# Attention backward on one core: loads and stores queued four at a time, the compute plan around them, a warm-up and halved last stores

## The chip, the cores and the metric

The kernel runs on one core of a Trainium2 chip. The metric is device time in microseconds (us): the median over executions of one build. Kernels that were executed once (the two repeats, those with loads and stores alone, the probes, many_dma, dense_dma, vec_dma, tag_before) have the state "unknown", since there is nothing to compare them with; their differences of some us are not backed by repeats. A profiled execution gives a span; it was 1.7 to 1.8 us shorter than the time of the same execution in the two profiles that are shown.

## The reference, cut to what matters

Attention with 32 query heads over 4 key/value heads, and its gradients. There are 32 batches; per batch `k` and `v` are 4 heads x 2048 keys x 128 in bf16, and `q`, `grad_out` are 32 heads x 4 queries x 128.

```python
def _fwd_reference(q, k, v):
    ...
    k = jnp.repeat(k, rep, axis=1)          # rep = 8 query heads share a key/value head
    v = jnp.repeat(v, rep, axis=1)
    scores = jnp.einsum("bhqd,bhkd->bhqk", q, k) * D ** -0.5
    p = _softmax(scores, axis=-1)
    return jnp.einsum("bhqk,bhkd->bhqd", p, v)

def reference(q, k, v, grad_out):
    ...
    _out, _vjp = jax.vjp(_f, q, k, v)
    return (out, dq, dk, dv)
```

Per batch the kernel reads K and V (4.2 MB) and writes dK and dV (4.2 MB); `q`, `grad_out`, the output and dQ are small and travel as an extra 256 bytes at the end of some rows. In all, 272.65 MB cross between memory and the chip's on-chip buffer (SBUF).

## The kernel before: the parts that the change touches

Everything is written out in advance. A string, `PLAN`, lists units of four characters: the name of the unit, its part, where it goes (PSUM bank, engine or slot) and a tile. The units are emitted in that order, so PLAN fixes the order on every engine. About 101 units make a batch.

Twenty "row slots" in SBUF hold both the rows that are loaded (K, V) and the rows that are to be stored (dV, dK). Per batch there are four loads and four stores of 128 rows each, of 8,192 bytes a row (LV0, LV1, SV0, SK0) or 8,448 bytes (LK0, LK1, SV1, SK1). All are issued by SyncE (SP), in order.

```python
SLOTS, E_TILES, DS_TILES = 20, 2, 2
NAMES = dict(a="LK", b="LV", ..., r="O", ..., u="DP", ..., y="DQ", ..., B="DVe", ..., D="DKe", E="SV", F="SK")
PLAN = ("a000a110b120a030b040a150e400f4A0e011f0A0..." ...)      # cut
...
    def emit(u):
        ...
        if name in ("LK", "LV"):                       # a load into slot u.where
            x = slots[int(u.where, 36)]
            ...
            for w in (slice(0, Sk), slice(Sk, n)) if b == 0 else (slice(0, n),):
                nc.sync.dma_start(out=x[:, w], in_=src[:, w])
        ...
        elif name in ("O", "DQ"):                      # 64 matmuls of 32 rows x 128 columns a batch, each
            ...
            for c in range(8):
                j, odd = divmod(c, 2)
                for h, r in enumerate(rows):
                    right = t[x, h].rearrange("p (j d e) -> p j d e", d=D, e=2)
                    nc.tensor.matmul(t[name][r, :], lhsT=left[:, j, r, odd], rhs=right[:, 4 * i + j, :, odd],
                                     start=(i == 0 and c == 0), stop=(i == 1 and c == 7), tile_position=(0, 32 * h))
        ...
        elif name in ("DVe", "DKe"):                   # eviction: PSUM -> the row that will be stored
            i, g = divmod(i, 2)
            copy = nc.scalar.copy if u.where == "A" else nc.vector.tensor_copy
            copy(out=heads_of(t[name[:2], "out", g])[:, :, QW * i:QW * i + QW],
                 in_=t[name[:2], i, g].rearrange("p (h c) -> p h c", h=2))
        elif name in ("SV", "SK"):                     # a store, from the slot
            n = LONG if i else ROW
            nc.sync.dma_start(out=(dv_r if name == "SV" else dk_r)[i][b], in_=t["D" + name[1], "out", i][:, 0:n])
```

In the plan before, loads and stores alternate. The order on the queue in each batch is `LV1 LK0' SK1 SV1 LV0 SV0 LK1' SK0` (a prime marks a later batch), and each store stands directly behind its last eviction.

At most eight DMAs were outstanding. DMA k was issued only when all of DMA k-8 had landed (of the 252 from the ninth on, none starts earlier): LK1 of batch 25 was issued at 482.6 us, the moment at which LK1 of batch 24, eight DMAs earlier, landed (482.6 us).

## Time and profile before

| | before |
|---|---|
| time, median of 3 | 672.78 us (672.17 to 672.86) |
| profiled span | 671.1 us |
| TensorE (PE) busy | 607.9 us, 91% |
| VectorE, ScalarE (DVE, ACT) busy | 572.0 and 569.6 us |
| data, at the usual packet time (309 ns for 8,192 bytes, on 16 engines 424 GB/s) | 643 us |

The first fence is from the page of the profile: busy time and count of each engine, the strips of the span in 40 equal slices (a digit is tenths of busy time; GB/s is what the DMA engines moved), the DMA queues (packets, MB, share of 16 engines) and the chain of work that ended last.

```profile
span 671.1 us, 20678 instructions
...
PE 607.9 (91%) x8768; PEld 401.4 (60%) x8768; DVE 572.0 (85%) x736; ACT 569.6 (85%) x802; POOL 39.0 (6%) x102
...
DMA  9999999999999999999999999999999999999867
GB/s 354 417 424 423 419 381 423 423 423 423 423 426 424 424 423 424 424 425 426 414 420 425 413 417 421 414 422 424 396 388 408 417 424 424 404 421 423 347 258 322
...
q1 hardware_dynamic: 37440, 272.65, 98.2%
q8 instruction: 69, 1.13, 0.6%
...
DMA 50%; PE 37%; DVE 4%; ACT 4%; issue 3%; SPq 0%; POOL 0%; DVEq 0%; ACTq 0%; POOLq 0%
```

Read it so: the DMA strip is full until the last three slices, the rate is 424 GB/s in a good slice, and half of the chain is DMA. The line `q8` is not data of the kernel: 69 packets of 16,384 bytes (the packet records give the size), which the page lists as of the kind "instruction".

### The profile page before, as it was taken

To read this page: it belongs to the slowest core of one execution; us is meant where nothing else is said; L and a number is where in the kernel's file an instruction comes from. 1 tells how busy PE (TensorE), PEld (TensorE's weight loads), DVE (VectorE), ACT (ScalarE), POOL (GpSimd) and SP (SyncE) were. 2 spreads that over 40 slices of the span, in tenths; PEclk is the share of its full clock that TensorE was granted. 3 is DMA by queue.
4 is the path that set the end of the run, shared out by engine and by line. 5 is a ranking of instruction groups with operands and counts; after the bars stand their busy time and mean duration, and the time that the engine had idled before them with its cause. 6 is when DMAs were issued, how large, how long until landed. Compare 5 with 4: busy or idle time off the path is not lost.

```text
span 671.1 us, 20678 instructions
## 1 busy us (share of the span) xinstructions
PE 607.9 (91%) x8768; PEld 401.4 (60%) x8768; DVE 572.0 (85%) x736; ACT 569.6 (85%) x802; POOL 39.0 (6%) x102
## 2 busy tenths in 40 slices
PE   6998999999998999988998989988999989898993
PEld 5665566666665666655655655655655666565651
DVE  1988799999997999988888989887888979896994
ACT  4997899999997999888888989887888979886894
POOL 0000000000000000000000000000000000000000
PEclk9999999999998999999999999998999989998997
DMA  9999999999999999999999999999999999999867
GB/s 354 417 424 423 419 381 423 423 423 423 423 426 424 424 423 424 424 425 426 414 420 425 413 417 421 414 422 424 396 388 408 417 424 424 404 421 423 347 258 322
DMA packets 37533, 273.97 MB, mean 408 GB/s; under 512 B 4160, under 2 KB 4160, under 8 KB 5184
## 3 DMA queue, kind: packets, MB, share of 16 engines
q1 hardware_dynamic: 37440, 272.65, 98.2%
q8 instruction: 69, 1.13, 0.6%
q14 instruction: 24, 0.20, 0.1%
HBM read 136.31 MB, written 136.31 MB: 406 GB/s over the span
## 4 chain that ended last, share of the span: by engine, by line
DMA 50%; PE 37%; DVE 4%; ACT 4%; issue 3%; SPq 0%; POOL 0%; DVEq 0%; ACTq 0%; POOLq 0%
DMA row<-in_k_dram 50%; PE psum L241 19%; PE psum L310 8%; PE psum L288 5%; PE psum L255 5%; ACT row L316 3%; DVE vt_sb L209 2%; DVE ds_sb L303 1%; DVE row L316 0%; DVE e_sb L260 0%; ACT e_sb L264 0%; PE psum L230 0%; SPq L226 0%; ACT dt_sb L207 0%; DVE row L296 0%
## 5 line engine op out<-in xcount | busy, mean ns | idle before, releaser
L241 PE MATMUL psum<-ident,row 128*128 128x128 f32 x2048 | 290.1, 284 | 28.4 <-DMA row<-in_k_dram 21.5
L316 ACT CAST row<-psum 128x1024 bf16<-128x1024 f32 x292 | 289.2, 1023 | 30.9 <-PE psum L310 29.1
L241 PEld LDWEIGHTS psum<-ident,row 128*128 128x128 f32 x2048 | 224.7, 143 | 94.8 <-issue 32.0
L316 DVE CAST row<-psum 128x1024 bf16<-128x1024 f32 x220 | 264.9, 1217 | 5.7 <-PE psum L310 2.9
L207 ACT COPY kt_sb<-psum 128x512 f32<-128x512 f32 x190 | 110.2, 598 | 20.6 <-PE psum L241 20.4
L207 ACT COPY vt_sb<-psum 128x512 f32<-128x512 f32 x160 | 92.0, 602 | 35.3 <-PE psum L241 34.6
L303 DVE SCALAR_TENSOR_TENSOR ds_sb<-psum,delta,e_sb 128x1024 bf16<-128x1024 f32 x64 | 82.1, 1283 | 13.4 <-PE psum L255 9.0
L310 PE MATMUL psum<-ds_sb,qp_sb 32*128 32x512 bf16 x512 | 76.9, 383 | 3.4 <-ACT row L316 1.0
L260 DVE TENSOR_SCALAR_CACHE_REDUCE e_sb<-psum 128x2048 bf16<-128x2048 f32 x32 | 73.3, 2292 | 5.7 <-PE psum L255 5.7
L310 PE MATMUL psum<-e_sb,dop_sb 32*128 32x512 bf16 x512 | 68.8, 388 | 2.5 <-issue 1.0
L209 DVE COPY kt_sb<-psum 128x1024 bf16<-128x1024 bf16 x66 | 45.0, 685 | 28.4 <-PE psum L241 27.8
L209 DVE COPY vt_sb<-psum 128x1024 bf16<-128x1024 bf16 x96 | 60.7, 684 | 10.0 <-PE psum L241 9.8
L264 ACT ACTIVATE e_sb<-psum,m 128x2048 bf16<-128x2048 f32 x32 | 64.0, 2001 | 0.2 <-DVE e_sb L260 0.2
L271 POOL TENSOR_SCALAR dop_sb<-row,rinv 128x128 bf16<-128x128 bf16 x32 | 19.3, 603 | 605.3 <-DVE rinv L268 530.3
L241 PE MATMUL psum<-ident,ds_sb 128*128 128x128 f32 x256 | 41.8, 286 | 9.6 <-DVE vt_sb L209 7.0
L288 PE MATMUL psum<-row,dt_sb 128*32 128x128 bf16 x2048 | 43.5, 222 | 6.2 <-issue 5.6
L310 PEld LDWEIGHTS <-qp_sb 32*128 32x128 bf16 x512 | 19.4, 91 | 46.1 <-issue 42.6
L255 PE MATMUL psum<-vt_sb,qdt_sb 128*32 128x512 bf16 x512 | 40.7, 388 | 4.6 <-issue 4.5
L288 PEld LDWEIGHTS <-dt_sb 128*32 128x32 bf16 x2048 | 30.8, 95 | 22.0 <-issue 21.1
L241 PEld LDWEIGHTS psum<-ident,ds_sb 128*128 128x128 f32 x256 | 26.9, 140 | 27.2 <-DVE vt_sb L209 16.4
L207 ACT COPY dt_sb<-psum 128x512 f32<-128x512 f32 x63 | 38.4, 611 | 1.0 <-PE psum L241 0.9
L288 PEld LDWEIGHTS <-et_sb 128*32 128x32 bf16 x2048 | 30.4, 95 | 13.8 <-ACT et_sb L207 11.3
(29 smaller groups left out, 310.1 us busy)
## 6 DMA issues: line engine op xcount, KB each, us to landing
out_dram<-row SPq DMA_DIRECT2D x64, 1056.0 KB, 20.1
out_dram<-row SPq DMA_DIRECT2D x64, 1024.0 KB, 20.4
row<-in_k_dram SPq DMA_DIRECT2D x62, 1056.0 KB, 18.1
row<-in_v_dram SPq DMA_DIRECT2D x62, 1024.0 KB, 20.5
row<-in_v_dram SPq DMA_DIRECT2D x4, 512.0 KB, 9.4
row<-in_k_dram SPq DMA_DIRECT2D x2, 544.0 KB, 5.3
row<-in_k_dram SPq DMA_DIRECT2D x2, 512.0 KB, 4.4
```

Of the source, the lines that this page charges most:

```text
L207: nc.scalar.copy(out=out.bitcast(FP32), in_=in_)
L209: nc.vector.tensor_copy(out=out, in_=in_.bitcast(BF16))
L241: nc.tensor.transpose(out=ps[:, P * j:P * j + P], in_=src[:, 4 * half + j, :], identity=ident32[:])
L255: nc.tensor.matmul(out[r, QW * w:QW * w + QW], lhsT=t["qdt"][:, P * side + 32 * h:P * side + 32 * h + 32], rhs=t[x, NH * i + h][:, QW * w: ...
L260: nc.vector.tensor_scalar(out=t["e"][:], in0=t["S"], scalar1=-scale, scalar2=None, op0=ALU.mult, op1=ALU.min, accum_out=t["m"][:])
L264: nc.scalar.activation(out=t["e"][:], in_=t["S"], func=ACT.Exp, bias=t["m"][:], scale=scale, accum_out=t["l"][:])
L271: nc.gpsimd.tensor_scalar(out=t["dop"][:], in0=t["go"], scalar1=t["rinv"][:], scalar2=None, op0=ALU.mult)
L288: nc.tensor.matmul(t[name][r, :], lhsT=left[:, j, r, odd], rhs=right[:, 4 * i + j, :, odd], start=(i == 0 and c == 0), stop=(i == 1 and c ...
L303: nc.vector.scalar_tensor_tensor(out=t["ds"][:, w], in0=t["DP", i], scalar=t["dl"][:], in1=t["e"][:, w], op0=ALU.subtract, op1=ALU.mult)
L310: nc.tensor.matmul(acc[:, QW * (h % 2):QW * (h % 2) + QW], lhsT=t[still][rows[h], :], rhs=t[moving][rows[h], QW * i:QW * i + QW], start=Tr ...
L316: copy(out=heads_of(t[name[:2], "out", g])[:, :, QW * i:QW * i + QW], in_=t[name[:2], i, g].rearrange("p (h c) -> p h c", h=2))
```

## The change

The intent, as far as the plan shows it: fewer changes of direction on the DMA queue. Four loads of a batch are queued in a row, then four stores: `LK0 LV0 LV1 LK1 | SV0 SV1 SK0 SK1`. Three of the four stores of a batch are held back for that (most of them 46, 70 or 91 units behind their last eviction, before: 1; SK1 still stands directly behind its last piece, the eviction of dQ), and compute is ordered anew, with long runs of the matmuls of O, DQ and DP placed where the loads run. Twenty transposes at the start are meant to warm PE up (in before the first 24 transposes took 228 to 243 ns each and the next 20, from 12.0 us on, 119), the first batch's loads are no longer halved, the last batch's stores are halved, and evictions write contiguous pieces. The diff, with the plan cut out:

```diff
+LAST = 31
+WARM_UP = 20
 ...
-PLAN = ("a000a110b120a030b040a150e400f4A0e011f0A0e702f7A0 ...")     # cut: all lines of the plan change
+PLAN = ("a000e000e111f1A0f0A0e422f4D0e533f5A0a110e744c050 ...")
 ...
+        if u.name in ("SV", "SK") and u.part > 1:
+            u.b = LAST
 ...
-            for w in (slice(0, Sk), slice(Sk, n)) if b == 0 else (slice(0, n),):
-                nc.sync.dma_start(out=x[:, w], in_=src[:, w])
+            nc.sync.dma_start(out=x[:, 0:n], in_=src)
 ...
-            copy(out=heads_of(t[name[:2], "out", g])[:, :, QW * i:QW * i + QW],
-                 in_=t[name[:2], i, g].rearrange("p (h c) -> p h c", h=2))
+            copy(out=t[name[:2], "out", g][:, 2 * QW * i:2 * QW * i + 2 * QW], in_=t[name[:2], i, g])
         elif name in ("SV", "SK"):
-            n = LONG if i else ROW
-            nc.sync.dma_start(out=(dv_r if name == "SV" else dk_r)[i][b], in_=t["D" + name[1], "out", i][:, 0:n])
+            half, g = divmod(i, 2)
+            n = LONG if g else ROW
+            w = (slice(0, n), slice(0, ROW // 2), slice(ROW // 2, n))[half]
+            nc.sync.dma_start(out=(dv_r if name == "SV" else dk_r)[g][b][:, w], in_=t["D" + name[1], "out", g][:, w])
 ...
+        for _ in range(WARM_UP):
+            nc.tensor.transpose(out=psum[:, QW * (BANKS - 1):QW * (BANKS - 1) + P], in_=ident32[:], identity=ident32[:])
```

The host's unpacking of dK and dV changes with the layout of the evictions. Slots are also reused sooner: a load follows the store that frees its slot by mostly 6 DMAs (before: 7 to 13), an eviction by mostly 5 or 6 (before: 9 to 14; the prediction counts one less, only the DMAs in between).

## The prediction

> **What bounds the kernel now.** The DMA engines. The page's strip shows them at 0.9 or more busy in 37 of 40 slices and about 424 GB/s in the good ones. The packet records agree: an 8192-byte packet takes 309 ns, on 16 engines 424 GB/s. [...] At that pace 272.65 MB take 643 us, of a span of 671.1. The compute engines have room: the starts of two successive exponentials lie 18.8 to 19.1 us apart where nothing stops them, against 20.1 us of DMA per batch; over most of the run the chain of waits is the DMA queue, about 20.5 us per batch.
>
> So at most some 28 us can go. I divide them by the packets' times:
> - start, 0 to 20 us: 3.0 us;
> - middle: about 11 us, nearly all of it packets that take longer than 309 ns, in bursts of 4 to 8 us (near 85-93, 475-480, 495-501 us) where the data rate falls by a fifth;
> - tail, from 620 us: 13.8 us, of which 12.5 are idle engines. The loads are over, the stores wait for evictions (timeline of the DMA queue's engine: one load at 619.3 us, then stores alone). The last store is issued at 663.1 us and waited for over 6.6 us.
>
> **What the change does.** Bytes, DMA count (apart from splits) and arithmetic stay. Evictions move between ACT and DVE, but with the measured durations (copies 0.60 and 0.69 us, casts 1.02 and 1.22 us) both engines' sums stay within 1%. The contiguous eviction target should not change a cast's time[...].
>
> 1. *Tail.* Counted in queue order at 424 GB/s, the last load ends at 610 us instead of 615 and the K loads of the last batch at 598 instead of 603: the last two batches' arithmetic starts about 5 us earlier. Half stores land sooner: the half loads at the start took 4.4 to 5.3 us, so the 6.6 us should become about 4.5. Gain 5 to 8 us.
> 2. *Start.* The transposes before 12 us take 228 to 243 ns each, later 119; the warm-up removes that. But the first load is no longer halved, and the DMA queue is full anyway: gain 0 to 1 us.
> 3. *Grouping.* Direction now changes twice per batch instead of some six times. Against it: where only loads ran (12 to 30 us) packets were about 1.3% over 309 ns, where only stores ran 2 to 3%, in the good mixed stretches 0.2%. For it: the bursts may come from mixing or from matmul runs meeting store reads; then part of 11 us goes. I expect these nearly to cancel: gain 0 to 6 us.
> 4. *Risk.* Slots are reused sooner (a load follows the store of its slot by 6 DMAs, before by 7 to 13; evictions into a slot follow its store by 4 or 5, before by 9 to 11), so compute waits for stores and the queue runs shallower; a loss only if it empties.
>
> **Prediction.** 662.5 us, 1.5% faster; 8 in 10 between 652 and 671. Chances: faster by over 2% 0.36, within 2% 0.59, slower by over 2% 0.05.
>
> **What would show it.** Tail: slices after 620 us above 340 GB/s on average, last store issued by about 658 us. Grouping: long packets in the middle fewer, or a common 313-317 ns pace in their place. Compute: exponentials still about 20.4 us apart or less, engine sums unchanged.
>
> **What would make it wrong.** Bursts vanish altogether (about 652), or the shallower queue empties each batch, or pure load and store phases are slower than read here (over 670).

A cast measured 1.02 us on ACT and 1.22 us on DVE in before and in after alike. Neither is a term of its sum, which stays as recorded: gains of 5 to 8, 0 to 1 and 0 to 6 us, together 5 to 15 us, and 662.5 us is some 10 us below before.

## More of the kernel before

The waits of SP, the issuer of all DMAs, say what held the queue back (total us, number of waits, longest):

```profile
SPq L320 <- DMA out_dram<-row: 125.1, 64, 2.2
SPq L226 <- DMA out_dram<-row: 105.4, 23, 5.6
SPq L320 <- DVE row L316: 89.1, 15, 9.3
```

Most of its waiting is for DMAs to land: in the first line for one of the eight places; in the second it is nearly always LK0, a load that waits for the store, seven DMAs ahead, that frees its slot. In the third a store stands at the head of the queue before its eviction is done. And the end of the run, by stage (length, busy time of each engine and number of instructions, granted clock, DMA share, GB/s):

```profile
600.00:640.00 40.00, 35.67 (x516) 23.88 (x515) 32.61 (x44) 32.18 (x45) 2.39 (x6) 0.96 0.94 392
640.00:671.10 31.10, 20.08 (x331) 11.48 (x329) 20.58 (x24) 21.60 (x29) 1.20 (x3) 0.89 0.68 278
642.00:646.00 4.00, 3.92 (x41) 2.64 (x40) 3.73 (x4) 3.44 (x7) 0.00 (x0) 1.00 0.74 304
646.00:650.00 4.00, 3.31 (x26) 1.83 (x25) 3.73 (x6) 4.00 (x6) 0.79 (x2) 1.00 0.09 34
```

From 640 us on the DMA engines are busy for only 68% of the time. The prediction took that as idle time to be won. The last of these lines already holds the answer, which I did not see at the time: from 646 to 650 us the DMA share is 0.09, a little over one engine of sixteen.

## The result, and the profile after

| | before | after |
|---|---|---|
| time, median of 4 runs of the same rounds | 672.47 us (671.41 to 672.86) | 676.75 us (676.19 to 678.05) |
| ratio | | 1.0069 (95% interval 1.0050 to 1.0088) |
| profiled span | 671.1 us | 674.9 us |

The kernel is slower, by about 4 us, and the interval excludes zero. Every ratio in this document is the mean time of one kernel's runs over the mean of the other's runs of the same rounds, so it is not quite the ratio of the medians that are quoted.

The page of after, the lines that answer to those shown of before:

```profile
span 674.9 us, 20722 instructions
...
PE 619.4 (92%) x8788; PEld 422.5 (63%) x8788; DVE 567.2 (84%) x760; ACT 575.3 (85%) x778; POOL 39.3 (6%) x102
...
DMA  9999999999999999999999999999999999999996
GB/s 365 420 418 423 389 424 423 422 425 427 422 422 424 425 423 423 418 398 411 419 402 425 409 416 412 412 424 407 415 416 392 389 424 358 422 403 343 344 422 280
...
q1 hardware_dynamic: 37440, 272.65, 98.7%
q8 instruction: 69, 1.13, 0.6%
...
PE 46%; DMA 34%; ACT 8%; DVE 5%; issue 5%; SPq 0%; POOL 0%; DVEq 0%; ACTq 0%
DMA out_dram<-row 29%; PE psum L244 24%; PE psum L313 10%; ACT row L319 6%; PE psum L291 6%; PE psum L258 5%; DMA row<-in_v_dram 3%; DMA row<-in_k_dram 2%; DVE vt_sb L214 2%; DVE row L319 1%; ACT row L297 1%; DVE ds_sb L306 1%; DVE e_sb L263 1%; PE psum L233 1%; DVE dt_sb L214 0%
```

The sums of DVE and ACT moved by 1% or less. PE's 11.5 us more go with a lower granted clock (the share of the full TensorE clock that the profile shows as allowed), 0.961 on average against 0.982: busy time times clock is 595 us here and 597 us before. The good slices still reach 424 GB/s, but there are fewer of them after the middle, and the share of the chain that is DMA is now stores (`out_dram<-row`), where it was loads before. The waits of SP and, new, waits of the two evicting engines for stores to land (there are none of these in before):

```profile
SPq L324 <- ACT row L297: 201.6, 27, 10.3
SPq L229 <- DMA out_dram<-row: 105.4, 46, 6.3
SPq L324 <- DVE row L319: 78.5, 27, 14.1
```

```profile
ACT row L319 <- DMA out_dram<-row: 24.3, 15, 2.2
...
DVE row L319 <- DMA out_dram<-row: 17.0, 15, 1.8
```

And the end by stage; the last load landed at 639.0 us (before: 640.1 us):

```profile
600.00:639.00 39.00, 38.16 (x556) 25.51 (x554) 33.57 (x45) 37.13 (x54) 2.20 (x5) 1.00 0.95 346
639.00:674.90 35.90, 22.88 (x409) 12.94 (x407) 22.99 (x29) 23.57 (x30) 1.42 (x4) 0.88 0.86 355
```

The tail is fuller than before (355 against 278 GB/s), exactly as the prediction wanted, and yet it is 4.8 us longer.

### Where the time is: the slowest of sixteen engines

The page averages over 16 DMA engines. The landings of the shares do not. The next table is worked out from them: for each DMA I took the time at which its last share landed, and from one DMA to the next the excess over 2.49 us (19.93 us a batch of eight DMAs, the pace that loads and stores alone kept, see below; half DMAs count half). It is thus the time that the slowest engine loses, waiting included, by the stage in which it loses it. That the sums come near to what the spans have over 643 us follows from the definition; what the table adds is where the time goes.

| us lost by the slowest engine, by stage of the span | 20-100 | 100-300 | 300-500 | 500-600 | 600-642 | from 642 | sum |
|---|---|---|---|---|---|---|---|
| before | 4.3 | 10.0 | 7.0 | 3.5 | 1.6 | 2.4 | 28.8 |
| before, second profile | 3.8 | 9.5 | 6.7 | 3.0 | 2.5 | 1.5 | 27.0 |
| after | 3.6 | 5.5 | 8.9 | 6.3 | 5.3 | 1.9 | 31.5 |
| after, second profile | 3.8 | 5.5 | 8.4 | 6.0 | 5.1 | 2.1 | 30.9 |
| loads and stores alone, order of before | 0.7 | 1.0 | 0.3 | 0.2 | -0.1 | 0.0 | 2.1 |

Three things follow.

First, the loss is no matter of a few bursts or of the two ends: in before it is 20.5 us over the 24 batches from 100 to 600 us, some 0.8 us a batch, where loads and stores alone lose 1.5 us. Second, after gains 4 to 4.5 us between 100 and 300 us, and gives back 7.3 to 8.4 us from 300 to 642 us. Third, the tail itself is not idle on that engine, in either kernel: from the last load's landing to the last store's, it works off its queue at 2.7 us a store, 11 stores before ((670.0 - 640.1) / 11 = 2.72) and 13 after ((673.8 - 639.0) / 13 = 2.68, the eight half stores counted as four). Before, the other engines are 7 to 13 us ahead of it (shares of the last load: first 626.6, fifteenth 632.8, last 640.1 us) and wait; that is the "idle" DMA time of the tail. From 642 us to the end that engine loses no more than 2.4 us in before: this is all that a better filled tail could have saved on it. The very last stores end nearly together on all engines (670.0 us on the slow one, 668.1 to 668.3 us on fourteen), since each is issued only when its evictions are done; so compute was close to being the limit there.

So after loads its last row 1.1 us earlier, but has two more stores still to do: 2 x 2.7 - 1.1 is 4.3 us, against 3.8 us of difference between the spans. This is bookkeeping and not yet a cause. The two stores merely changed places with loads: at the same place of the queue, 245 whole DMAs, the last share landed at 640.1 us in before and at 644.5 us in after. The time was lost before the tail.

Spread of the landings: in before, the distance from the first to the last share of a DMA grows from 2.3 us (batch 4) to about 12.8 us (batch 16) and stays there. From there on nearly each DMA is issued when the slowest engine frees a place, so all engines go at its pace (20.7 us a batch from batch 16 to 27, first and last share alike). In after the spread stays at about 7 us (5 to 9).

### The profile page after: what moved, and what is told of

Same layout as the page of the kernel before. It is cut to its first block, busy times and chain, and to the rows that moved or that the text cites. A ratio compares the mean times of both kernels' runs of the same rounds, so it can differ in the third digit from the quotient of the medians. Undisturbed runs are those within 1.5% of the kernel's fastest.

```text
span 674.9 us, 20722 instructions
## 1 busy us (share of the span) xinstructions
PE 619.4 (92%) x8788; PEld 422.5 (63%) x8788; DVE 567.2 (84%) x760; ACT 575.3 (85%) x778; POOL 39.3 (6%) x102
## 4 chain that ended last, share of the span: by engine, by line
PE 46%; DMA 34%; ACT 8%; DVE 5%; issue 5%; SPq 0%; POOL 0%; DVEq 0%; ACTq 0%
DMA out_dram<-row 29%; PE psum L244 24%; PE psum L313 10%; ACT row L319 6%; PE psum L291 6%; PE psum L258 5%; DMA row<-in_v_dram 3%; DMA row<-in_k_dram 2%; DVE vt_sb L214 2%; DVE row L319 1%; ACT row L297 1%; DVE ds_sb L306 1%; DVE e_sb L263 1%; PE psum L233 1%; DVE dt_sb L214 0%
## 5 line engine op out<-in xcount | busy, mean ns | idle before, releaser
L319 ACT CAST row<-psum 128x1024 bf16<-128x1024 f32 x349 | 341.8, 1022 | 46.5 <-DMA out_dram<-row 24.3
L244 PEld LDWEIGHTS psum<-ident,row 128*128 128x128 f32 x2048 | 233.5, 146 | 68.3 <-ACT row L319 33.4
L319 DVE CAST row<-psum 128x1024 bf16<-128x1024 f32 x163 | 197.9, 1219 | 21.1 <-DMA out_dram<-row 17.0
L214 DVE COPY kt_sb<-psum 128x1024 bf16<-128x1024 bf16 x117 | 80.2, 687 | 32.2 <-PE psum L244 21.5
L214 DVE COPY vt_sb<-psum 128x1024 bf16<-128x1024 bf16 x149 | 97.6, 685 | 11.0 <-PE psum L244 9.8
L313 PE MATMUL psum<-e_sb,dop_sb 32*128 32x512 bf16 x512 | 83.3, 398 | 19.8 <-ACT row L319 19.5
L212 ACT COPY kt_sb<-psum 128x512 f32<-128x512 f32 x139 | 79.6, 597 | 20.2 <-PE psum L244 20.0
L212 ACT COPY vt_sb<-psum 128x512 f32<-128x512 f32 x107 | 60.2, 599 | 7.4 <-PE psum L244 6.2
L313 PEld LDWEIGHTS <-dop_sb 32*128 32x128 bf16 x512 | 23.8, 92 | 51.8 <-issue 40.8
L291 PEld LDWEIGHTS <-dt_sb 128*32 128x32 bf16 x2048 | 33.8, 95 | 11.5 <-issue 6.7
L244 PE MATMUL psum<-ident,e_sb 128*128 128x128 f32 x256 | 39.4, 280 | 0.0
## 6 DMA issues: line engine op xcount, KB each, us to landing
out_dram<-row SPq DMA_DIRECT2D x62, 1056.0 KB, 12.8
```

What stands on the lines that cost most here:

```text
L212: nc.scalar.copy(out=out.bitcast(FP32), in_=in_)
L214: nc.vector.tensor_copy(out=out, in_=in_.bitcast(BF16))
L244: nc.tensor.transpose(out=ps[:, P * j:P * j + P], in_=src[:, 4 * half + j, :], identity=ident32[:])
L313: nc.tensor.matmul(acc[:, QW * (h % 2):QW * (h % 2) + QW], lhsT=t[still][rows[h], :], rhs=t[moving][rows[h], QW * i:QW * i + QW], start=Tr ...
L319: copy(out=t[name[:2], "out", g][:, 2 * QW * i:2 * QW * i + 2 * QW], in_=t[name[:2], i, g])
```

## The experiments

A letter for a theory holds for the runs of its own section; the theories changed as they fell. Eighteen kernels were run.

### 1. Chance or program: the two kernels again

> The kernel before once more, to see whether the stretched packets are a property of the program or chance. If they come from what the program does (addresses, order, slots), the same DMAs are slow again: the K loads of batches 18 to 23 and 25 to 27, and the excess over 309 ns per 8192 bytes sums to about 13.8 us per engine. If they come from outside, other DMAs are slow and the sum differs by some us. About 672 us either way.

> The changed kernel once more. If the program makes the stretched packets: again about 21 us per engine, and again the second K load (LK1) of every other batch from 16 on and the last store of every other batch. If chance: other DMAs, another sum. About 677 us.

Measured, on one chip: 671.88 us and 675.82 us. The second profiles lose their time in the same stages as the first (table above) and at the same DMAs (correlation of the losses, DMA by DMA from the 17th to the 250th: 0.82 for before, 0.92 for after), and the same two loads of batches 30 and 31 are late in both profiles of after. The difference belongs to the program.

### 2. The order of the DMAs alone

Each kernel cut down to its loads and stores, in its own order and slots; no compute, results wrong.

```diff
-    units = plan()
+    units = [u for u in plan() if u.name in ("LK", "LV", "SV", "SK")]     # as a plan of 256 or 260 units; slots are set to zero first
```

> The loads and stores of the kernel before alone, in its order and slots, no compute (wrong results on purpose). Theory Q (the order of the DMA queue, by itself, decides the rate): about 660 us, with the stretched packets still there. Theory C (the compute engines' accesses or their waits make the losses): 643 us of packets plus 3 to 5 us at the ends, 646 to 652 us, with almost no stretched packets.

> The loads and stores of the changed kernel alone, grouped four and four, no compute (wrong results on purpose). Theory Q: slower than the same for the kernel before by 4 us or more, because grouping stretches packets. Theory C: the same as that run within 2 us, so that the loss of the changed kernel arises in the interplay with compute (slots that are freed late, evictions that wait for stores).

Measured: 647.15 us and 649.83 us, 25 us less than with compute. The page of the first:

```profile
span 645.4 us, 365 instructions
...
GB/s 335 424 426 421 428 425 427 425 428 425 428 426 428 428 429 426 425 428 427 429 427 427 428 428 428 428 426 428 427 428 427 428 427 428 428 427 429 427 428 339
...
q1 hardware_dynamic: 37440, 272.65, 100.4%
q14 instruction: 2, 0.02, 0.0%
```

All 16 engines keep one pace, 19.93 us a batch. So the DMA engines did the whole job in spans of 645 and 648 us. After's order costs 2.5 us here, all of it in the first 300 us (the slowest engine loses 4.7 us up to 300 us, against 1.7 us in the order of before); its sooner reuse of slots is part of that run too, so this is not grouping alone, and each of the two kernels was executed once. And some 25 us of both kernels come from the presence of compute. The line of instruction fetches of PE, `q8`, is gone.

### 3. Are the held-back stores the cost?

After, with each store moved to directly behind its last eviction (89 stores moved, nothing else).

> The changed kernel with each store moved in the DMA queue to right behind its last eviction (91 stores or fewer move; nothing else). Theory H (stores are held back until the four loads are queued, so that finished outputs keep their slots and evictions and loads wait for stores that have not landed): the 41 us in which ACT and DVE wait for a store shrink below 10 us and the time falls to 668 us or less. Theory D (the order of directions itself is what costs): still grouped three and three, so within 2 us of 676.7. Theory P (packets are stretched by what compute does at the same moment): the sum of stretched time changes with the phase, up or down, and the time with it.

Measured: 732.39 us, ratio 1.0882 (1.0849 to 1.0916). The theory that holding the stores back costs time is refuted for this order of loads; there it saves 56 us. What happens instead is in SP's waits:

```profile
SPq L324 <- DVE row L319: 424.8, 62, 20.3
SPq L324 <- ACT row L319: 97.9, 57, 16.9
```

SP stands at a store whose eviction is not done, and the loads behind it in the queue wait with it. With four loads in a row, the loads have to come before stores that are not ready.

### 4. Grouping alone

Before, with three of the four loads of a batch moved to a later place so that four loads and four stores stand in a row; slots and compute untouched.

> The kernel before with three of four loads moved later in the DMA queue, so that four loads and four stores follow one another, slots and compute order untouched; a load follows the store of its slot by 12 to 18 DMAs. Theory D (grouping itself costs): 3 us or more slower than before, stretched time above 16 us against 13.8. Theory H: within 1.5 us of before, since no slot becomes tight.

Measured: 684.53 us, ratio 1.0181 (1.0161 to 1.0202). In the compute order of before, this grouping costs 12 us. It also brings three loads of each batch later, and the run does not separate the two. By the landings, the last load lands at 650.5 us instead of 640.1, and the rest takes 31.6 us instead of 31.0, so the loss lies before the tail. If grouping costs as much in after, its new compute order recovers most of it; that is a comparison, not a test.

### 5. Does one kind of matmul take the bandwidth?

The DMA stream of each kernel, with PE working through long runs of one kind of matmul after the other (S, O, DV, transposes), then evictions. Their outputs are wrong, which doesn't matter for the times.

> The DMAs of the kernel before alone, while the compute engines run one kind of work after the other on tiles of their own, without any wait on the DMAs (wrong results on purpose): about 100 us of S-type matmuls, 100 of O-type, then DV-type, transposes, evictions. Theory P (a kind of matmul or eviction takes SBUF or other bandwidth from the DMA engines): in one of these stretches the packets take well over 309 ns and the data rate falls by 10 per cent or more. Otherwise none of the stretches differs from the DMAs alone (0.76 us stretched in 500) and the time is 645 to 650 us.

> The same probe with the DMA order of the changed kernel, loads and stores in separate phases of 10 us. Theory P: the stretching in the affected stretch follows the direction, loads or stores, and shows which of the two suffers. Otherwise as the DMAs alone, 648 to 652 us.

Measured: 736.34 and 735.84 us, set by the evictions at the end, so the time says nothing. The DMA stream is what counts: its last share landed at 666 and 669 us, against 644 and 647 us without compute. The slowest engine lost 1 to 4 us in each 60 us of PE's work after 40 us, whatever its kind, and in the probe of before only 0.4 us after PE's work had ended (526 us). No kind of matmul stood out. That PE's work costs the DMA engines some 22 us, whatever the work is, was the new fact.

### 6. What of PE's work costs? Many small instructions, or few large ones

Here I rebuilt, from the packet records, which packets belong to one DMA engine: on a busy engine of these records a packet starts 3 or 4 ns before the one ahead of it ends, and the shares of the DMAs follow in order. For the run of loads and stores alone this puts exactly 2,340 packets on each of 16 chains. In before and after it shows two things that the page does not: the 69 fetch packets lie on eight of the engines in turn (in before a fetch took its engine 0.88 to 1.38 us, median 0.94, and the packet behind it some 0.4 us over its pace), and one other engine has many small delays of 2 to 40 ns (16 to 18 us in sum in the two profiles of before, 17.4 us in the second of after; each of the other 15 under 1.5 us).

Four kernels. The first two are the loads and stores of before with a stream of matmuls that wait for nothing:

```python
        for n in range(13800):                                     # many_dma: 32 x 32, 64 columns moved
            h = n % 4
            nc.tensor.matmul(psum[rows[h], ...], lhsT=vt[rows[0], 0:32], rhs=e[rows[0], 0:64], start=True, stop=True,
                             tile_position=(0, 32 * h))
        for n in range(3000):                                      # dense_dma: 128 x 128, 512 columns moved
            nc.tensor.matmul(psum[...], lhsT=vt[:, 0:P], rhs=e[...], start=True, stop=True)
```

> Only the loads and stores of the kernel before, in its order, plus 13,800 tiny matmuls on PE (32 rows by 32 columns, 64 columns moved) that wait for nothing; results wrong on purpose. Chaining the DMA packets of the run of before by their times puts each 16,384-byte instruction-fetch packet on one of eight of the sixteen engines in turn, and each costs that engine about 0.95 us plus about 0.4 us on the packet behind it. Theory F (instruction fetch slows the DMA engines): about 108 fetches, 13 or 14 on each of eight engines at about 1.3 us, so the last landing moves from 643.9 us (loads and stores alone) to 655-664 us, with no one engine that stands out by many small delays of 5 to 40 ns. Theory D (dense streaming of PE, not the number of its instructions, slows one single engine by many small delays): that signature is missing here (sum of delays of 2 to 40 ns under 5 us on every engine).

> The same loads and stores, plus 3,000 matmuls of 128 by 128 with 512 columns moved[...], so that PE streams for some 640 us with few instructions. Theory F: about 23 fetches, 3 on each of eight engines, last landing at most 649 us. Theory D: one engine alone shows small delays (2 to 40 ns a packet) of 15 us or more in sum, as one engine did in the profiles of before (16 to 18 us) and after (about 17 us), the other fifteen under 3 us, and the last landing is at 658 us or later, with the other engines some 10 us ahead or held back by it.

The third halves the number of matmuls of O and DQ in before, with PE as long at work (busy 606.6 us, before 607.9; wrong):

```diff
-            for c in range(8):
-                j, odd = divmod(c, 2)
+            for j in range(4):
                 for h, r in enumerate(rows):
-                    right = t[x, h].rearrange("p (j d e) -> p j d e", d=D, e=2)
-                    nc.tensor.matmul(t[name][r, :], lhsT=left[:, j, r, odd], rhs=right[:, 4 * i + j, :, odd], ...
+                    right = t[x, h].rearrange("p (j d) -> p j d", d=2 * D)
+                    nc.tensor.matmul(t[name, "wide"][r, :], lhsT=left[:, j, r, 0], rhs=right[:, 4 * i + j, :], ...
```

> The kernel before with the 32x128 products of O and DQ issued in pairs: half as many matmuls of O and DQ with 256 columns moved instead of 128, so PE streams as long with about 23 per cent fewer instructions; O and DQ are wrong on purpose. Theory F as the bound: fetches fall from 69 to about 53, the time falls by 3 to 5 us to 667.5-669.5 us. Theory D as the bound (the slow engine is not one that fetches): within 1 us of before (671.5-673.5 us), with 16 to 18 us of small delays still on one engine.

The fourth is after with whole last stores; it belongs to section 8.

Measured: many_dma 685.47 us (its last share landed at 682.3 us), dense_dma 668.36 us (PE ends last; its last share landed at 650.7 us), half_before 667.56 us, ratio 0.9924 (0.9908 to 0.9941). The fetch lines of the two streams, many_dma first:

```profile
q8 instruction: 107, 1.75, 0.9%
```

```profile
q8 instruction: 23, 0.38, 0.2%
```

PE was busy for 649.4 us in dense_dma (97%) and for 204.1 us in many_dma (30%), and many_dma cost the DMA stream 38 us, dense_dma 6. So in these two runs it is the number of instructions (27,967 against 6,367), not the streaming. Neither theory was right in its figures. (half_before's 667.56 us lies in the range of theory F, but that number does not speak for fetches: they fell from 69 to 52 together with the instructions, and in the two streams another engine ended last.) The fetch theory gave many_dma 655 to 664 us: the eight engines with fetches did end late, at 671 to 677 us, but one engine without any fetch ended last, at 682. In dense_dma the eight engines with two or three fetches each ended at 645 to 647 us, against 641 to 643 for those without: about 1.3 us for each fetch. And one engine without fetches ended at 650.7 us.

That one engine is the bound in these runs. Its small delays (2 to 320 ns a packet over the pace of 309 ns), and the median of the 16 engines for comparison:

| run | instructions | slow engine, us | median engine, us | difference for each instruction |
|---|---|---|---|---|
| loads and stores alone | 365 | 2.8 | 1.8 | |
| dense_dma | 6,367 | 10.1 | 1.8 | 1.3 ns |
| vec_dma (below) | 9,367 | 21.1 | 8.0 | 1.4 ns |
| half_before (to 630 us) | 16,582 | 20.7 | 2.2 | 1.1 ns |
| before, second profile | 20,678 | 25.9 | 4.9 | 1.0 ns |
| many_dma | 27,967 | 37.4 | 6.9 | 1.1 ns |

In half_before the loss of the slowest engine over the whole run fell to 23.1 us, from 27.0 and 28.8 us, while its instructions fell to 0.80. About 2 us of the gain came before 100 us, at a place where before has a stop of its own, so the gain of 5 us isn't all the slow engine's pace.

### 7. Any instruction, or PE's? And which engine?

vec_dma: the loads and stores with 6,000 tiny DVE copies and 3,000 tiny ACT copies, no PE. tag_before: before, with 15 small extra loads of 1, 2, ... 15 rows amid batches 10 to 16, each with its own packet size.

```diff
+                if 80 <= count < 140 and count % 4 == 0:
+                    n = (count - 80) // 4 + 1
+                    w = slice(0, 64 + 4 * n)
+                    nc.sync.dma_start(out=junk[0:n, w], in_=k_r[0][0, 0:n, w])
```

> The loads and stores of the kernel before alone, plus 6,000 tiny DVE copies and 3,000 tiny ACT copies and no PE instruction. The two PE streams cost one engine 1.3 to 1.4 ns for each instruction of the program (27,967 instructions: about 39 us; 6,367: 9 us). Theory N (every instruction of any engine costs that one DMA engine about 1.35 ns): one engine falls 11 to 14 us behind the quickest ones. Theory D2 (only PE's instructions do): no engine falls behind by more than the share of the fetch packets (about 35 of them, 4 to 5 on each of eight engines, 5 to 6 us).

> The kernel before with 15 small extra loads amid batches 10 to 16, of 1 to 15 rows, each of its own packet size, so that the chains of packets can be told apart by number: an engine whose chain holds a packet of the load of n rows is one of the engines that such a load uses. [...] the sixteen chains hold 0, 1, 2 ... 15 such packets, one chain each, and the one chain with 15 us or more of small delays gets a number. If the tags do not spread so, the slow engine stays unnumbered. Time within 2 us of before.

Measured: vec_dma 701.63 us, its last share at 692.1 us, 48 us later than with loads and stores alone; the expectation had nothing of that size. One engine has the small delays here too (12.5 us between 2 and 40 ns, the others at most 2; by the table 13 us more than the median engine, as theory N said), so DVE's and ACT's instructions count about as PE's do here (1.4 ns each in the table, against 1.0 to 1.3 ns in the runs with PE). But another engine ended last. Fetches of DVE and ACT are listed in another queue:

```profile
DVE 587.2 (84%) x6022; ACT 590.7 (84%) x3001; POOL 0.7 (0%) x6
...
q1 hardware_dynamic: 37440, 272.65, 97.2%
q14 instruction: 72, 0.59, 0.2%
```

72 packets of 8,192 bytes. In the chains, 47 of them lie on one DMA engine and 23 on one other, for 6,000 instructions of DVE and 3,000 of ACT: 128 and 130 for each packet. Read so, all fetches of DVE went to one DMA engine in this run, and all of ACT to another. The engine with the 47 was the last, some 7 us behind the next. In before the page lists only 24 such packets (0.1% of the engines' time), so this is no limit there.

tag_before took 682.58 us, 10 us more, not the 2 us expected: 15 small loads in the queue of eight hurt. But the tags did put engines in an order. In the chains up to 255 us, the packets of the loads of 1, 2, 3, 4 and 5 rows lie nested (the load of 1 row on one chain, that of 2 on the same and one more, and so on), and the chain with the small delays holds a packet of the load of 5 rows and none of the smaller ones: it is the fifth engine in the order in which these loads take them up. The eight engines with PE's fetches hold none of these tags. The nested tags of 1 to 5 rows are what was measured. The chains broke off at 255 us (too many stops), so the tags of 6 to 15 rows are not read.

### 8. Which part of the change costs the 4 us?

whole_after: after, with the last batch's four stores whole, each where its second half stood.

> The kernel after with the last batch's four stores whole again, each where its second half stood. Prediction's step 1 (halved last stores shorten the tail): 1 to 3 us slower than after, 677.5-680 us. If the end is set by the one slow engine that has to work off its lag, the halves are worth little: 676-677.5 us, within 1 us of after.

Measured: 676.70 us, ratio to before 1.0062 (1.0047 to 1.0077), as after (1.0069). The halved stores are worth nothing here.

shallow_before: before, with only the letters of the slots in the plan changed, so that slots are reused about as soon as in after.

> The kernel before with its compute and its order of loads and stores untouched and only the row slots chosen otherwise: a load reuses a slot 6 or 7 DMAs after the store that frees it (before: 7 to 13), an eviction 5 to 7 DMAs after (before: 9 to 14); after has 6 and 5 to 6. If the shorter reuse of slots is what costs the kernel after its 4 us: 674.5-680 us here, ratio above 1.003. If it is not: 671.5-673.5 us, ratio 0.998 to 1.002.

Measured: 692.86 us, ratio 1.0281 (1.0249 to 1.0313). Twenty us from the choice of slots alone. The waits that came with it, and the chain:

```profile
DVE row L316 <- DMA out_dram<-row: 35.4, 19, 2.6
```

```profile
DMA out_dram<-row 32%; PE psum L241 23%; PE psum L310 7%; ACT row L316 7%; PE psum L255 7%; DVE vt_sb L209 5%; DVE row L316 4%; PE psum L288 4%; ACT kt_sb L207 2%; DMA row<-in_k_dram 1%; DVE ds_sb L303 1%; ACT e_sb L264 0%; ACT dt_sb L207 0%; DVE e_sb L260 0%; DVE row L296 0%
```

This is the mark that after carries too: evictions that wait for a store to land, stores in the chain where loads were, and a queue that is not full. One thing differs: in after 47 of the 54 loads that follow a store in their slot start within 0.03 us of the landing of that store's last share, mostly six DMAs ahead, so that at most six are outstanding at that moment; in before it is 22 (within 0.1 us, seven DMAs ahead), in shallow_before none, where evictions alone are held. Worked out from issues and landings between 340 and 600 us, the slowest engine has 7.8 DMAs outstanding in before, 6.3 in after, 5.8 in shallow_before; the spread of the landings is 13, 7 and 6 us.

mix_after: after's compute, with the stores directly behind their evictions and the loads mixed among them as in before, slots chosen anew.

> The kernel after with its compute order, its contiguous evictions, its warm-up and its halved last stores, but each store directly behind its last eviction and the loads mixed among the stores as in before, slots chosen anew with reuse 7 to 12 DMAs behind a store. If the queue order and slot reuse are the cause of the loss: back to 670-673.5 us. If the new compute order is the cause: 675 us or more.

Measured: 697.88 us, ratio 1.0377 (1.0359 to 1.0395). By the letter of the expectation this puts the loss on the compute order, but I don't conclude that: a plan tuned for one queue order was given another, and ACT waited 60.3 us for stores to land, more than in after (24.3 us). It is inconclusive for the question.

half_after: after, with O and DQ in pairs as in half_before.

> The kernel after with the products of O and DQ issued in pairs as in half_before (about 4,100 fewer PE instructions, PE streams as long, O and DQ wrong on purpose). If after, too, is limited by the DMA engine that loses 1.3 to 1.4 ns for each instruction: 5 to 7 us less than after, 669.5-672 us, the same step as half_before made from before (5.0 us). If after is limited by its own waits (evictions and loads held up by stores) rather than by that engine: at most 2 us less, 674.5-677 us.

Measured: 675.43 us, ratio to before 1.0052 (1.0032 to 1.0072). Against after (676.75 us, another batch of runs) that is about 1 us, where before had gained 5. So after has limits of its own on top. The landings show where one of them is. In after, in its second profile and in half_after alike, the slowest engine loses 1.4 to 2 us at each of two loads near the end: LV0 of batch 30 (4.3 to 4.5 us behind the landing before it, instead of 2.5) and LV1 of batch 31 (4.0 to 4.4 us). Both were issued late. The timeline of SP in after shows why (start, duration, engine, line, operation), and so do its waits from 606 to 632 us:

```profile
612.04 0.34 SPq L229 DMA_DIRECT2D row<-in_v_dram  x1
...
616.58 0.33 SPq L229 DMA_DIRECT2D row<-in_v_dram  x1
617.00 11.48 SPq L324 DMA_DIRECT2D out_dram<-row  x2
628.53 1.62 SPq L229 DMA_DIRECT2D row<-in_v_dram  x1
```

```profile
SPq L324 <- DVE row L299: 21.6, 2, 11.0
SPq L229 <- DMA out_dram<-row: 7.4, 2, 5.1
```

LV0 of batch 30 is the load at 612.04 us. Its slot is freed by SK0 of batch 27, only three DMAs ahead, whose last share landed at 612.02 us: here the sooner reuse of a slot holds up a load. At 617 us two stores are at the head of the queue. The second is SK1 of batch 28, whose last piece (dQ, line 299) is evicted only at 628 us. The last load of the kernel stands behind it and gets its turn at 628.5 us; it then waits for something itself (the profile names PE), and its issue ends at 630.1 us. In before the last load was issued at 619.3 us. SP waits for the dQ piece in nearly every batch (there ACT evicts it, line 297: 201.6 us in 27 waits in the fence of the result); what that costs earlier in the run was not tested.

### 9. A version with fewer instructions that computes the right thing

pairdq_before: DQ by 32 matmuls of 64 rows and 256 columns a batch instead of 64 of 32 rows and 128 columns; two heads share a matmul, half of what it makes is not used, and four small evictions take the blocks.

```diff
+                    for g in range(2):
+                        r = slice(64 * g, 64 * g + 64)
+                        right = t[x, "pair", g].rearrange("p (h j d e) -> p j e h d", h=2, d=D, e=2)
+                        nc.tensor.matmul(t[name][r, :].rearrange("p (h d) -> p h d", h=2), lhsT=left[:, j, r, odd],
+                                         rhs=right[:, 4 * i + j, odd], ..., tile_position=(0, 64 * g))
```

> A version of before with right results: DQ is made by 32 products of 64 rows and 256 columns a batch instead of 64 of 32 rows and 128 columns; half of each result is not used, and four small evictions a batch take the useful blocks. 2,048 PE instructions fewer, 96 ACT and DVE instructions more. At 1.35 ns for each instruction the slow engine gains 2.6 us: 669.5-671 us, ratio 0.9955 to 0.998, if PE[...] stays off the path. If PE or the evictions hold it up: 672 us or more.

Measured: correct, 688.24 us, ratio 1.0248 (1.0232 to 1.0264): the second outcome of the expectation, and by more than I had thought (an estimate of PE's extra work is cut there, as it names no measurement; the figure is below). The chain has left the DMA queue:

```profile
PE 636.6 (93%) x7744; PEld 419.0 (61%) x7744; DVE 578.4 (84%) x768; ACT 594.6 (87%) x866; POOL 39.2 (6%) x102
...
PE 62%; DVE 17%; ACT 12%; issue 4%; DMA 3%; DVEq 0%; ACTq 0%; SPq 0%
```

PE has 29 us more to do (636.6 against 607.9 us) and is 93% busy; compute is now the bound. No version that beats the kernel before came out.

## Why the prediction was wrong, point by point

**"What bounds the kernel now. The DMA engines."** Right, but read too coarsely. The bound is one engine of sixteen. "So at most some 28 us can go" is where the account failed first: it treats the distance from the ideal as loss in three separate places (start, bursts of long packets, idle tail) that a better order could remove. The landings show one place for most of it: the slowest engine loses 27 to 29 us over the run of before and about 31 us over that of after, and the loads and stores of before alone lose 2 us in the same order. That the long packets on the fast engines are their waiting for work that the slow one has not yet let SP issue is likely, but not shown.

**Step 1, "Tail. ... Gain 5 to 8 us."** This is the step that failed. "12.5 are idle engines" was true of the mean, not of the engine that ends last, which worked through the tail without a gap at 2.7 us a store and lost only 2.4 us after 642 us. The last load did not land 5 us earlier but 1.1 us: on its way the queue lost 2.6 to 3.7 us more than in before between 600 and 642 us, most of it at two loads, one held by the store of its slot and one behind a store that was not ready (read from the timeline; no run moved these loads). And 13 rows of stores instead of 11 were left behind it. Measured: the rest after the last load takes 35.9 us instead of 31.0. Half stores: nothing (whole_after, 676.70 against 676.75 us).

**Step 2, "Start ... gain 0 to 1 us."** Right. By packet time, 0 to 20 us lost 2.5 us instead of 3.0.

**Step 3, "Grouping ... gain 0 to 6 us."** Wrong in sign, as far as it was tested. After's order costs 2.5 us in the DMA stream alone, and grouping costs 12 us in before's compute order. The packets over 10% long rose from 804 to 1,217 instead of falling.

**Step 4, "Risk ... a loss only if it empties."** The mechanism was named and its condition was wrong. The queue needn't empty. With 7.8 DMAs outstanding on the slowest engine (before) the landings of a DMA were spread over 13 us, with 6.3 (after) over 7, with 5.8 (shallow_before) over 6. My reading is that the depth lets the fifteen other engines run ahead of the slow one, and lets loads be issued in time. shallow_before took 20 us more with nothing but the slots changed. That the 7 to 8 us which after loses more from 300 us on have this cause is argued from the same marks (waits of evictions for stores, 41 us in 30 waits against none; 47 loads that start at the landing of their slot's store; 6.3 DMAs outstanding), not shown by a run that gives after a deeper queue.

**"What would show it."** "Slices after 620 us above 340 GB/s" came true (353 GB/s against 310) without any gain. It was a bad sign to choose: the tail with more stores left was the fuller one (13 stores, 355 GB/s, against 11 and 278). "Last store issued by about 658 us" failed (664.7 us). "Exponentials still about 20.4 us apart": 20.3 us in both kernels, the sums of DVE and ACT within 1%, as said.

**What stays open.** Why after loses 4 to 4.5 us less than before from 100 to 300 us. Whether the lower granted clock of after (0.958 to 0.970 in its four runs, 0.975 to 0.993 in the runs of before beside the experiments) has a part in the loss: no run tests it, but from 600 to 639 us, where after falls behind by some 3 us, it had 1.00, against 0.96 in before up to 640 us. What that fifth DMA engine does for each instruction; no packet in the records stands for it. All runs here were recorded, so none shows whether it belongs to running or to recording a program. Whether after with its last load put ahead of SK1 of batch 28 would gain anything, as that load had a wait of its own until 630.1 us, and whether rows could be taken away from that engine, was not tried.

## What to carry to other kernels

When DMA engines are the bound, look at the landing of the last share of each DMA, not at the mean share of busy time: in the tail of before the 16 engines were busy for only 68% of the time on average, and the one that ended last lost no more than 2.4 us there. Before a queue is reordered, count for each slot how many DMAs lie between the store that frees it and its next use, and look for loads that stand behind stores which are not ready; both cost more here (20 us, 56 us) than any gain from direction changes. And near the DMA limit instructions were not free here: each one cost 1.0 to 1.4 ns on one DMA engine.
